# A hand-made instruction scheduler with the price of array shape changes by direction, traced durations, and a search over the finished order

## The chip, the cores and the metric

The kernel runs on one NeuronCore of a Trainium2 chip. Engines work side by side, each in the order of its own queue, and wait for each other by semaphores: TensorE (PE, matmuls; PEld is its weight load), VectorE (DVE), ScalarE (ACT), GpSimd (POOL) and SyncE (SP), which here issues nearly all DMA transfers. The metric is device time of one execution in microseconds (us), median of several runs.

## What is computed

A retention layer for 8 batches and 8 heads (sequence 576, head size 64) and, on its result, a two-layer network with a PReLU between.

```python
scores = scale * np.matmul(q, k.transpose(0, 1, 3, 2))
gamma = 1.0 - 2.0 ** (-5.0 - np.arange(H, dtype=np.float32))
Dmat = np.where(rel >= 0, gamma[:, None, None] ** rel[None, :, :], 0.0)
ret = scores * Dmat[None, :, :, :]
attn_out = np.matmul(ret, v)              # (8, 8, 576, 64)
x = attn_out.transpose(0, 2, 1, 3).reshape(4608, 512)
h = x @ w_in                              # (4608, 2048)
g = np.maximum(h, 0.0) + alpha * np.minimum(h, 0.0)
return g @ w_out                          # (4608, 512)
```

## The kernel before

**The work.** The attention is done in chunks of 64 positions. The first two batches go by `part_...` functions (all heads of a stretch at once), the other 24 pairs of batch and two heads by `joint` (L893): one joint computes scores and states of pair n (small matmuls of 64x64 at L913, L920, L923, one scheduler operation called "su") and the values of pair n-1 (128x64 matmuls at L861, two operations "v0" and "v1"). "su" fills the PSUM banks psa, the values fill psh. DVE masks the scores into the tile `at` (L941), ACT and DVE add up the states (`su`, L953 to L964), and SP's transfers copy qT into `at` and the states `su` into `vn`. Sixteen transfers belong to a joint, loads of the next pairs among them.

The network works on blocks of 256 tokens and slices of 256 hidden units. For 32 bits of precision each operand is split into three pieces (`h`, `l`, `d`; `split_g`, `split_roll`, `split_w`), and the products of pieces add up in PSUM. `unit_roll` (L1188) and `unit_two` (L1222) make the hidden units, in psh for one half of a slice and in psa for the other; `second` (L1340) multiplies by w_out into the banks pso; `evacuate` writes `o` (DVE L1358, L1363) and sends it out through SP. While weights are still on their way, the first eight cells use whole fp32 operands instead (`unit_plain` L1091, `second_plain` L1122); `convert` (L711) turns the 64-bit weights into fp32 on ACT, DVE and POOL. At about 440 us the attention is finished, and what follows are 128x512 matmuls alone.

**The order.** Nothing is issued as the functions are called. `do` records an `Op`: its engine, a cost in us that is written beside it, the operations that it depends on, the PSUM banks, whether it holds the port that DVE and POOL share (`lock`), its number of PE instructions (`size`), and a `kind` (for PE: "small" for 64-wide matmuls, "pieces" for the split 128x512 ones, "PE" for the rest). `dues` (L232) lays all operations out backwards from the end and so gives each a due time. `plan` (L266) goes forwards: for each engine it takes, among the ready operations that could start within a small slack of the earliest, the one with the least due time. A change of kind on PE costs a flat 0.1 us:

```python
SLACK, SWITCH = {"PE": 0.2}, {"PE": 0.1}
return t + SWITCH.get(op.eng, 0.0) * (kinds[op.eng] != op.kind)
```

A transfer is also held back by `plan` until its due time less 30 us, and until no more than 2 us of transfers are queued. Blocks of 256 PE instructions are modelled as fetched in 3.1 us (`CHUNK`, `FETCH`). Twelve rounds of `dues` and `plan` and then 243 random shifts of due times in stretches of 40 us keep the plan that ends first. Its order is issued on all engines; dependencies between holders of the port, and a limit on bytes in flight during the first 100 us, are added on the way. Costs and due times live only in this planning; the chip sees the order of each queue and the waits.

Of the kernel before, what the change touches and what calls it, by code (L numbers as in the profile page):

```python
# [1 line left out]

# [19 lines left out]
def kernel(  # L22
# [130 lines left out]
    ops, land = [], [LAND[0]]  # L153
# [48 lines left out]
        return op  # L202


    RATE, RATE_256, RATE_128 = 265e3, 205e3, 115e3

    def dma(to, fro, size, r, w, eng="SP", rate=RATE, hold=0.0):
        def f():
# [23 lines left out]
    def dues(after):  # L232
# [30 lines left out]
                    ready[d.eng].append(d)  # L263
        return due

    def plan(due):  # L266
        last = -min(due)
        left = [len(op.deps) for op in ops]
        ready = {e: [] for e in BEGIN}
        rest = [op.n for op in ops if op.eng == "PE"]  # L270
        end, begin, order = [0.0] * len(ops), [0.0] * len(ops), []
        free, held, port, wire, kinds = dict(BEGIN), {}, [0.0, ""], 0.0, {e: e for e in BEGIN}
        can = [0.0] * len(ops)

        at = [CHUNK - 190, 0.0]
        for op in ops:
            if not op.deps:
                ready[op.eng].append(op)

        def earliest(op):  # L280
            t = max(free[op.eng], can[op.n], op.hold)
            for b in op.banks:
                if b in held:
                    t = max(t, max([x + LAT.get(e, 0.1) for e, x in held[b].items()
                                    if e != op.eng] or [0.0]))
            if op.lock and port[1] != op.eng:
                t = max(t, port[0])
            if op.late:
                t = max(t, wire - BACKLOG, due[op.n] + last - HOLD)
            if op.size and at[0] + op.size > CHUNK:  # L290
                t = max(t, at[1] - op.cost * (CHUNK - at[0]) / op.size)
            return t + SWITCH.get(op.eng, 0.0) * (kinds[op.eng] != op.kind)

        while len(order) < len(ops):
            pick = None
            for e, queue in ready.items():
                if not queue:
                    continue
                c = [(earliest(op), op) for op in queue
                     if e != "PE" or op.n <= rest[0] + AHEAD_PE]  # L300
                if not c:
                    continue
                t0 = min(t for t, _ in c)
                t, op = min((x for x in c if x[0] <= t0 + SLACK.get(e, 0.05)),
                            key=lambda x: (due[x[1].n], x[1].n))
                if pick is None or t < pick[0]:
                    pick = t, op
            t, op = pick
            ready[op.eng].remove(op)
            if op.eng == "PE":  # L310
                rest.remove(op.n)
            begin[op.n] = t
            kinds[op.eng] = op.kind
            free[op.eng] = end[op.n] = t + op.cost
            if op.size:
                at[0] += op.size
                if at[0] >= CHUNK:
                    at[0] -= CHUNK
                    over = end[op.n] - op.cost * at[0] / op.size
                    at[1] = over + FETCH + min(max(wire - over, 0.0), 0.8)  # L320
            if op.late:
                wire = max(wire, t + op.cost) + op.late
# [12 lines left out]
        total = max(end)  # L335
        return total, order, begin, end

    AHEAD_PE = 150
    WINDOWS, STRETCH, TRIES, ROUNDS = 27, 20.0, 9, 9
    CHUNK, FETCH = 256, 3.1  # L340
    BACKLOG, HOLD = 2.0, 30.0
    LAG, HOLD_X = 2, 100.0
    X_TWO, QUICK, NQUICK, WDVE = 12, 13, 2, 16
# [1 line left out]
    EARLY, JOINTS = 1, {(s, i): 1 for s in range(14) for i in range(2) if (s, i) not in ((0, 0), (8, 1), (10, 1), (13, 0), (13, 1))}  # L345
    PUMP0, PUMP = ((1, 2), (0, 1), (0, 1), (0, 1)), ((1, 2), (1, 2), (0, 1), (0, 1))
    GROUPS = (("v0",), ("v1",), ("x", "su"))
    SLACK, SWITCH = {"PE": 0.2}, {"PE": 0.1}
    BEGIN = {"PE": 1.9, "ACT": 0.5, "DVE": 5.5, "POOL": 5.4, "SP": 0.5}


# [137 lines left out]
    def part_scores(x, bank):  # L489
# [7 lines left out]
        for m in range(2):  # L497
            def f(m=m):
                for c in range(NPAIR):
                    for p2 in range(2):  # L500
                        for h2 in range(2):
                            j = chunk(2 * m + p2)
                            nc.tensor.matmul(
                                ps[h2].get()[half(p2), (2 * c + m) * C:(2 * c + m + 1) * C],
                                kT()[half(h2), c, j], qT()[half(h2), c, j], start=True, stop=True)
            do("PE", 0.58, f, [(kt, "t", m), (qt, "t", m)], [(ps[0], m), (ps[1], m)], kind="small",
               size=64)
        for h2 in range(2):
            def g(h2=h2):
# [6 lines left out]
    def part_states(x, bank):  # L516
# [4 lines left out]
        for m in range(2):  # L521
            def f(m=m):
                for c in range(NPAIR):
                    for p2 in range(2):
                        for h2 in range(2):
# [3 lines left out]
                                             start=(m == 0 and c == 0),  # L529
                                             stop=(m == 1 and c == NPAIR - 1),  # L530
                                             skip_group_check=True)
            do("PE", 0.58, f, [key_p(x, 0, m), key_p(x, 2, m)], [(pu[0], 0), (pu[1], 0)], kind="small",
               size=64)
        for j in range(4):
            was = sums_key(x, j - 1) if j else carry_key(x) if x % 3 else None
# [24 lines left out]
    def part_values(x, bank):  # L560
# [7 lines left out]
        for m in range(2):  # L568
            def f(m=m):
                for c in range(NPAIR):  # L570
                    for p2 in range(2):
                        for h2 in range(2):
# [6 lines left out]
            do("PE", 0.58, f, [key_p(x, 2, m), (a, "m", 0), (a, "m", 1)], [(pv[0], 0), (pv[1], 0)],  # L579
               kind="small", size=64)  # L580


# [55 lines left out]
    def last_part(x):  # L638
# [28 lines left out]
        do("PE", 0.6, f, [(t, "t")], [(ps[0], 0), (ps[1], 0)], kind="small", size=32)  # L667
# [6 lines left out]
        def f():  # L674
# [6 lines left out]
            for c in range(NPAIR):  # L681
                for h2 in range(2):
                    for e in range(0, D, 32):
# [4 lines left out]
        do("PE", 1.25, f, [key_p(x, 2, 0), (t, "m", 0), (t, "m", 1), (t, "t"), carry_key(x)], [(pv, 0)],  # L688
           kind="small", size=96)
        gx, o = chunk_home(x, NJ - 1)  # L690
        do("ACT", 0.37, lambda: nc.scalar.copy(
# [158 lines left out]
    def values(n, pv):  # L850
# [6 lines left out]
        for i, js in enumerate((range(0, j1), range(j1, NJ))):  # L857
            def f(i=i, js=js):
                for j in js:
                    for h2 in range(2):  # L860
                        nc.tensor.matmul(pv[i].get()[half(h2), (j - js[0]) * C:(j - js[0] + 1) * C],  # L861
                                         vns[n % 2][:, h2, j], mt.get()[:, h2, j], start=True,
                                         stop=True)
            parts.append((0.133 * len(js), f, [(vn, x, h2) for x in "vs" for h2 in range(2)] +
                          [(mt, x, h2) for h2 in range(2) for x in ("q", "s", "x")],
                          [(pv[i], 0)]))
        return parts, lambda: keep_x(n, pv, j1)
# [18 lines left out]
    def on_pe(parts, groups):  # L886
        for some in groups:
            do("PE", sum(parts[x][0] for x in some), lambda some=some: [parts[x][1]() for x in some],
               [key for x in some for key in parts[x][2]],
               [key for x in some for key in parts[x][3]], kind="small",  # L890
               size=sum(136 if x == "su" else 72 if x[0] == "v" else 0 for x in some))

    def joint(n):  # L893
# [23 lines left out]
        def f():  # L917
            for j in range(NJ - 1):
                for h2 in range(2):
# [3 lines left out]
                    nc.tensor.matmul(chunks(uu)[half(h2), j], kn.get()[half(1 - h2), j],  # L923
                                     vns[n % 2][half(1 - h2), h2, j], start=True, stop=True,
                                     skip_group_check=True)
        parts["su"] = (1.09, f, [(kT, 0), (qT, 0), (kn, 0), (kn, 1), (vn, "v", 0), (vn, "v", 1)],
                       [(ss, 0), (uu, 0), (uu, 1)])
        on_pe(parts, [some for some in ([x for x in group if x in parts] for group in GROUPS)
                      if some])
# [90 lines left out]
    def split_x(vis, rooms=None, side=0):  # L1020
# [23 lines left out]
        late = vis["n"] >= LATE_X and rooms is None  # L1044
        for n in range(2):
            for c in parts(n, (0,)):
                do("ACT", 0.64 if len(c) > 1 else 0.38,
                   lambda c=c, to=view(0, c): nc.scalar.mul(piece(to()), raw(c), BELOW * 2.0 ** -12),
                   keys, key(0, c))
            for c in parts(n, (0, 1, 2)):  # L1050
# [8 lines left out]
                        out=piece(l()), in0=raw(c), in1=ht(), op=ALU.subtract),  # L1059
                        keys + [(h, 0)], key(1, c))  # L1060
                else:
                    do("ACT", 0.64 if wide else 0.38,
                       lambda c=c, d=d: nc.scalar.mul(piece(d()), raw(c), BELOW), keys, key(2, c))
# [5 lines left out]
                do("POOL", 1.29 if wide else 0.7,  # L1069
                   lambda l=l, d=d, h=view(0, c): nc.gpsimd.tensor_tensor(  # L1070
                       out=piece(d()), in0=h(), in1=l(), op=ALU.subtract),
                   key(0, c) + key(1, c), key(2, c), lock=True)
# [139 lines left out]
    def unit_two(va, vb, u, outs, f):  # L1212
# [3 lines left out]
        def mm():  # L1216
            for p, l in ((p0, 0), (p1, 2), (p0, 1)):
                for cc in range(NCC):
# [5 lines left out]
        do("PE", 2.73, mm, x_keys(va, 0) + x_keys(vb, 1) +  # L1224
           [w_at[u, i][l] for i in range(2) for l in range(3)], [(p0, 0), (p1, 0)], size=24, kind="pieces")
        fc = 2 * u + f
        for cols, gens, g in outs:
# [97 lines left out]
    def second(cell):  # L1325
# [7 lines left out]
        for m in range(2):  # L1333

            terms = ((0, 0), (0, 1)), ((1, 2),)
            for some in reversed(terms) if cell["last"] else (sum(terms, ()),):
                def mm(m=m, a=list(acc), some=some):
                    for f in range(2):
                        for b, l in some:
# [2 lines left out]
                                             w_piece(u, 2 + f, l),  # L1342
                                             start=(cell["first"] and f == 0 and l != 1),
                                             stop=(cell["last"] and f == 1 and l > 0))
                do("PE", 0.459 * len(some), mm, [(g, l) for _, l in some] +
                   [w_at[u, i][l] for i in (2, 3) for _, l in some],
                   [(acc[2 * m + b], 0) for b in sorted({b for b, _ in some})], size=4 * len(some), kind="pieces")
            if cell["last"]:
# [349 lines left out]
    for n in range(ROUNDS * WINDOWS):  # L1698
# [6 lines left out]
        if made[0] <= best[0]:  # L1705
            best, due = made, other

    port = None
    for op in best[1]:
        now[0] = best[2][op.n]  # L1710
        ins = op.fn()
        if op.lock:
            if port and port[0] != op.eng:
# [34 lines left out]
```

## Time and profile before

| | us |
|---|---|
| median of 3 runs | 918.88 (918.88 to 920.27) |
| profiled execution | 919.19 |
| its span | 917.4 |
| PE busy | 906.9 |
| PE weight loads (PEld) busy | 737.8 |
| DVE / ACT / POOL busy | 548.0 / 503.9 / 520.2 |
| data moved by DMA | 121.32 MB |

The span is the time from the first to the last instruction of the profiled execution. A line of the order of time gives start, duration, engine, source line, operation, output tile and input tiles, shapes and a count; in square brackets stands how long the engine was idle before it and what ended that. Rows are merged where the same instruction repeats, so their durations overlap: the time between two starts is the time that PE took. A row of stretches gives the stretch, its length, and for PE, PEld, DVE, ACT and POOL the busy time and (x) the number of instructions, then the clock granted to PE as a share of full speed, the busy share of the DMA engines and GB/s.

These groups take most of PE's time:

```profile
L1340 PE MATMUL pso<-w,g 128*128 128x512 f32 x1392 | 338.8, 391 | 0.0
L1188 PE MATMUL psh<-lx_x,w 128*128 128x512 f32 (+1 forms) x360 | 86.6, 379 | 0.0
L1188 PE MATMUL psa<-lx_x,w 128*128 128x512 f32 (+1 forms) x360 | 85.4, 376 | 0.0
```

### The profile page before, as it was taken

To read this page: it belongs to the slowest core of one execution; us is meant where nothing else is said; L and a number is where in the kernel's file an instruction comes from. 1 tells how busy PE (TensorE), PEld (TensorE's weight loads), DVE (VectorE), ACT (ScalarE), POOL (GpSimd) and SP (SyncE) were. 2 spreads that over 40 slices of the span, in tenths; PEclk is the share of its full clock that TensorE was granted. 3 is DMA by queue.
4 is the path that set the end of the run, shared out by engine and by line. 5 is a ranking of instruction groups with operands and counts; after the bars stand their busy time and mean duration, and the time that the engine had idled before them with its cause. 6 is when DMAs were issued, how large, how long until landed. Compare 5 with 4: busy or idle time off the path is not lost. (4 is left out here: it accounts for less than half of the span.)

```text
span 917.4 us, 19097 instructions
## 1 busy us (share of the span) xinstructions
PE 906.9 (99%) x7289; PEld 737.8 (80%) x7289; DVE 548.0 (60%) x1003; ACT 503.9 (55%) x1010; POOL 520.2 (57%) x461
## 2 busy tenths in 40 slices
PE   7999999999999999999999999999999999999998
PEld 6767688887888888888888888888888888888886
DVE  5786766667677667676757776344444534344343
ACT  4575455646565656565746555537463636364441
POOL 4776746456466665674542244665656656574624
PEclk9999999999999999999999999999999999999999
DMA  9995688977988879895243332212121322211112
GB/s 216 251 235 86 164 189 186 198 178 155 221 192 194 209 166 201 193 189 181 93 138 130 102 125 65 86 57 81 58 89 56 99 73 86 74 64 47 47 46 69
DMA packets 235947, 121.32 MB, mean 132 GB/s; under 512 B 203456, under 2 KB 203728, under 8 KB 235856
## 3 DMA queue, kind: packets, MB, share of 16 engines
q1 hardware_dynamic: 235712, 119.98, 52.1%
q8 instruction: 57, 0.93, 0.4%
q14 instruction: 34, 0.28, 0.1%
q10 hardware_dynamic: 144, 0.13, 0.0%
HBM read 74.19 MB, written 32.51 MB: 116 GB/s over the span
## 5 line engine op out<-in xcount | busy, mean ns | idle before, releaser
L1340 PE MATMUL pso<-w,g 128*128 128x512 f32 x1392 | 338.8, 391 | 0.0
L1340 PEld LDWEIGHTS pso<-w,g 128*128 128x128 f32 x1392 | 258.9, 188 | 55.2 <-POOL g L1267 1.2
L1264 POOL TENSOR_TENSOR g<-ga_all,g 128x512 fp32r<-128x512 f32 x76 | 97.9, 1291 | 130.4 <-ACT g L1260 105.0
L1267 POOL TENSOR_TENSOR g<-g 128x512 fp32r<-128x512 f32 x114 | 147.4, 1294 | 23.7 <-DVE su L1066 5.7
L1188 PE MATMUL psh<-lx_x,w 128*128 128x512 f32 (+1 forms) x360 | 86.6, 379 | 0.0
L1188 PE MATMUL psa<-lx_x,w 128*128 128x512 f32 (+1 forms) x360 | 85.4, 376 | 0.0
L1188 PEld LDWEIGHTS psa<-lx_x,w 128*128 128x128 f32 x360 | 65.1, 188 | 13.1 <-issue 0.4
L1188 PEld LDWEIGHTS psh<-lx_x,w 128*128 128x128 f32 x360 | 64.2, 188 | 12.9
L1260 ACT ACTIVATE g<-ga_all 128x512 fp32r<-128x512 f32 x76 | 47.6, 631 | 43.0 <-PE pso L1340 21.0
L1256 POOL TENSOR_TENSOR g<-g 128x512 fp32r<-128x512 f32 x22 | 28.5, 1296 | 64.0 <-DVE g L1253 38.3
L1264 POOL TENSOR_TENSOR g<-vn,g 128x512 fp32r<-128x512 f32 x25 | 32.4, 1297 | 37.5 <-ACT g L1260 34.9
L1340 PE MATMUL pso<-lx_x,g 128*128 128x512 f32 x216 | 53.5, 390 | 0.1
L1163 POOL TENSOR_TENSOR lx_x<-lx_x 128x512 fp32r<-128x512 f32 x28 | 35.9, 1294 | 26.0 <-DVE lx_x L1160 26.0
L941 DVE SCALAR_TENSOR_TENSOR at<-psa,pf,mask 64x512 f32<-64x512 f32 x48 | 36.0, 749 | 21.1 <-PE psh L861 10.2
L1340 PEld LDWEIGHTS pso<-lx_x,g 128*128 128x128 f32 x216 | 40.4, 188 | 9.0 <-DVE o L1363 0.7
L1262 ACT ACTIVATE g<-ga_all 128x512 fp32r<-128x512 f32 x76 | 47.2, 621 | 0.0
L1358 DVE TENSOR_TENSOR op<-pso,op 128x512 f32<-128x512 f32 x35 | 24.0, 686 | 31.3 <-PE pso L1340 31.2
L1202 ACT COPY ga_all<-psh 128x512 f32<-128x512 f32 (+1 forms) x30 | 16.7, 558 | 39.1 <-PE psh L1188 37.4
L861 PEld LDWEIGHTS psh<-at,vn 128*64 128x64 f32 x864 | 27.9, 137 | 8.7 <-issue 3.6
L1222 PE MATMUL psh<-w,w 128*128 128x512 f32 x144 | 34.6, 389 | 0.0
L1222 PE MATMUL psa<-w,w 128*128 128x512 f32 x144 | 34.6, 389 | 0.0
L754 POOL TENSOR_TENSOR wa<-wa,op 128x512 int32<-128x512 int32 x16 | 21.0, 1311 | 23.1 <-DVE wa L751 19.1
(329 smaller groups left out, 1883.3 us busy)
## 6 DMA issues: line engine op xcount, KB each, us to landing
xk<-x SPq DMA_DIRECT2D x18, 512.0 KB, 3.7
ok<-o SPq DMA_DIRECT2D x36, 256.0 KB, 2.9
op<-ok SPq DMA_DIRECT2D x18, 512.0 KB, 3.9
out_dram<-o SPq DMA_DIRECT2D x35, 256.0 KB, 2.3
x<-xk SPq DMA_DIRECT2D x16, 512.0 KB, 5.6
qx<-in_q_dram SPq DMA_DIRECT2D x96, 72.0 KB, 3.4
kx<-in_k_dram SPq DMA_DIRECT2D x96, 72.0 KB, 3.3
kn<-in_k_dram SPq DMA_DIRECT2D x48, 144.0 KB, 3.4
```

Of the source, the lines that this page charges most:

```text
L861: nc.tensor.matmul(pv[i].get()[half(h2), (j - js[0]) * C:(j - js[0] + 1) * C], vns[n % 2][:, h2, j], mt.get()[:, h2, j], start=True, stop= ...
L941: nc.vector.scalar_tensor_tensor(out=mt.get()[half(1 - h2), h2, j], in0=fro[x], scalar=pf[x, 1, h:h + 1], in1=mask[x, None, :].to_broadcas ...
L1163: do("POOL", 1.29, lambda h=h, l=l, d=d: nc.gpsimd.tensor_tensor(out=piece(d()), in0=h(), in1=l(), op=ALU.subtract), [(g, 0, n), (g, 1, n) ...
L1188: nc.tensor.matmul(out_of(p), w[:, c0:c0 + P], xp(l, cc), start=(l != 1 and cc == 0), stop=(l > 0 and cc == NCC - 1))
L1222: nc.tensor.matmul(p.get(), w[:, c0:c0 + P], piece(words_of(g)[:, o:o + DM]), start=(l != 1 and cc == 0), stop=(l > 0 and cc == NCC - 1))
L1256: do("POOL", 1.29, lambda: nc.gpsimd.tensor_tensor(out=piece(to.get()[:, 2]), in0=to.get()[:, 0], in1=to.get()[:, 1], op=ALU.subtract), [( ...
L1260: do("ACT", 0.64, lambda: nc.scalar.mul(piece(to.get()[:, 2]), whole(), BELOW), both, [(to, 2)])
L1262: do("ACT", 0.64, lambda: nc.scalar.mul(piece(to.get()[:, 0]), whole(), BELOW * 2.0 ** -12), both, [(to, 0)])
L1264: do("POOL", 1.29, lambda: nc.gpsimd.tensor_tensor(out=piece(to.get()[:, 1]), in0=whole(), in1=to.get()[:, 2], op=ALU.subtract), both + [( ...
L1267: do("POOL", 1.29, lambda: nc.gpsimd.tensor_tensor(out=piece(to.get()[:, 2]), in0=to.get()[:, 0], in1=to.get()[:, 1], op=ALU.subtract), [( ...
L1340: nc.tensor.matmul(a[2 * m + b].get(), piece(g.get()[:, l, f, m * P:(m + 1) * P]), w_piece(u, 2 + f, l), start=(cell["first"] and f == 0 a ...
L1358: do("DVE", 0.69, lambda: nc.vector.tensor_tensor(out=t(), in0=p1.get(), in1=t(), op=ALU.subtract), [(p1, 0)], [tk])
```

## The change

Three things. First, a change of kind on PE has a price by direction: from a large kind ("PE", "pieces") to a small one 0.09, from a small one to a large one 0.24, among small ones 0.1, between the two large kinds nothing. The values become a kind of their own ("values"). Second, costs are set to other figures: small matmuls, values, the split products, some narrow ACT and POOL operations, the rates of transfers. Third, `mend` takes the order that `plan` found. It replays a whole order of all engines with fixed positions, and tries 30000 moves of one operation to an earlier or later place. In 15% of them it puts a small PE operation next to another small one; in the others it picks a gap on PE, walks back along what caused it, and pulls an operation forward or pushes the one ahead of it back. A move stays if the measure, the end plus 0.3 times the mean start of PE's operations, is no worse. The replay has the fetch of instruction blocks, the banks, the port and the transfers' wire; it does not hold transfers back as `plan` does, and neither does the issue. `now`, which decides what the limit on bytes in flight is applied to, comes from the replay's start times. The arithmetic is untouched.

```diff
-    RATE, RATE_256, RATE_128 = 265e3, 205e3, 115e3
+    RATE, RATE_256, RATE_128 = 272e3, 211e3, 119e3
...
+    def switch(a, b):
+        if a == b or a in BIG and b in BIG:
+            return 0.0
+        return OUT if b in BIG else INTO if a in BIG else AMONG
...
-            return t + SWITCH.get(op.eng, 0.0) * (kinds[op.eng] != op.kind)
+            return t + switch(kinds[op.eng], op.kind)
...
+    def mend(order):
...
+        def earlier(x, p):
+            p = max([p] + [pos[d] + 1 for d, _ in needs[x]])
+            return p < pos[x] and (order[:p] + [x] + order[p:pos[x]] + order[pos[x] + 1:], p, pos[x])
+
+        def later(x, p):
+            p, q = min([p, num - 1] + [pos[u] - 1 for u in uses[x]]), pos[x]
+            return p > q and (order[:q] + order[q + 1:p + 1] + [x] + order[p + 1:], q, p)
+
+        def proposal():
+            if rnd.random() < 0.15:
+                x = rnd.choice(some)
+                by, p, seen = rnd.choice((1, -1)), pos[x], 0
+                while seen < 14:
+                    p += by
+                    if not 0 <= p < num:
+                        return None
+                    if eng[order[p]] == pe:
+                        if small[order[p]]:
+                            return seen and (later(x, p - 1) if by > 0 else earlier(x, p + 1))
+                        seen += 1
+                return None
+            if not idle or rnd.random() < 0.02:
+                idle[:] = gaps()
+            x = rnd.choices(idle, [min(g, 1.0) for g, _ in idle])[0][1]
+            for _ in range(rnd.randrange(25)):
+                w = why[x] if why[x] >= 0 else before[x] if why[x] == -1 else (
+                    locked[x] if why[x] == -3 else -1)
+                if w < 0:
+                    break
+                x = w
+            y = before[x] if rnd.random() < 0.7 or not ops[x].lock else locked[x]
+            for _ in range(rnd.choice((0, 0, 0, 1, 1, 2, 3, 4))):
+                y = before[y] if y >= 0 and before[y] >= 0 else y
+            if y < 0:
+                return None
+            if rnd.random() < 0.5:
+                return earlier(x, pos[y])
+            return later(y, pos[x] + rnd.choice((0, 0, 0, 5, 10, 20, 40)))
...
+        def worth(total, begin):
+            return total + 0.3 * sum(begin[n] for n in on_pe) / len(on_pe)
+        value = worth(total, begin)
+        for _ in range(MOVES):
+            change = proposal()
+            if not change:
+                continue
+            other, first, last = change
+            k = first // MARK
+            b, e, w, m = begin[:], end[:], why[:], dict(marks)
+            t = replay(other, k * MARK, marks[k], b, e, w, m, (marks, end), last + 1)
+            if t is None:
+                continue
+            v = worth(t or total, b)
+            if v <= value:
+                order, begin, end, why, marks = other, b, e, w, m
+                total, value = t or total, v
+                index()
+        return order, begin, total
...
+    MARK, FAR, WORSE, MOVES = 64, 192, 0.3, 30000
...
-    SLACK, SWITCH = {"PE": 0.2}, {"PE": 0.1}
+    SLACK, BIG, INTO, OUT, AMONG = {"PE": 0.2}, ("PE", "pieces"), 0.09, 0.24, 0.1
...
-            do("PE", 0.58, f, [(kt, "t", m), (qt, "t", m)], [(ps[0], m), (ps[1], m)], kind="small",
+            do("PE", 0.49, f, [(kt, "t", m), (qt, "t", m)], [(ps[0], m), (ps[1], m)], kind="small",
...
-            parts.append((0.133 * len(js), f, [(vn, x, h2) for x in "vs" for h2 in range(2)] +
+            parts.append((0.117 * len(js), f, [(vn, x, h2) for x in "vs" for h2 in range(2)] +
...
-               [key for x in some for key in parts[x][3]], kind="small",
+               [key for x in some for key in parts[x][3]], kind="values" if some[0][0] == "v" else "small",
...
-        parts["su"] = (1.09, f, [(kT, 0), (qT, 0), (kn, 0), (kn, 1), (vn, "v", 0), (vn, "v", 1)],
+        parts["su"] = (1.07, f, [(kT, 0), (qT, 0), (kn, 0), (kn, 1), (vn, "v", 0), (vn, "v", 1)],
...
-                do("PE", 0.459 * len(some), mm, [(g, l) for _, l in some] +
+                do("PE", 0.4545 * len(some), mm, [(g, l) for _, l in some] +
...
+    mended = mend([op.n for op in best[1]])
     port = None
-    for op in best[1]:
-        now[0] = best[2][op.n]
+    for n in mended[0]:
+        op = ops[n]
+        now[0] = mended[1][n]
         ins = op.fn()
```

More of the change, by code (lines that the diff above doesn't have):

```diff
@@ L1 @@
+import random
 from contextlib import ExitStack
@@ L336, in plan, with replay, index, gaps @@
         return total, order, begin, end
+    def mend(order):
+        num, rnd = len(ops), random.Random(1)
+        engs = list(BEGIN)
+        pe = engs.index("PE")
+        eng = [engs.index(op.eng) for op in ops]
+        kind = [op.kind for op in ops]
+        small = [op.eng == "PE" and op.kind not in BIG for op in ops]
+        kinds = {k for e, k in zip(eng, kind) if e == pe} | {"PE"}
+        turn = {(a, b): switch(a, b) for a in kinds for b in kinds}
+        lat = [LAT.get(e, 0.1) for e in engs]
+        needs = [[(d.n, wait(d, op)) for d in op.deps] for op in ops]
+        uses = [[u.n for u in users[op.n]] for op in ops]
+        on_pe = [n for n in range(num) if eng[n] == pe]
+        some = [n for n in on_pe if small[n]]
+        def replay(order, at, state, begin, end, why, marks, was=None, same=0):
+            free, port, side, wire, a0, a1, kd, held = state
+            free, held = list(free), {b: dict(v) for b, v in held.items()}
+            for p in range(at, num):
+                if p % MARK == 0:
+                    st = list(free), port, side, wire, a0, a1, kd, {b: dict(v) for b, v in held.items()}
+                    if was and p >= same:
+                        if st == was[0][p // MARK] and all(
+                                end[m] == was[1][m] or all(pos[u] < p for u in uses[m])
+                                for m in order[at:p]):
+                            return 0.0
+                        if p >= same + FAR and free[pe] > was[0][p // MARK][0][pe] + WORSE:
+                            return None
+                    marks[p // MARK] = st
+                n = order[p]
+                op, e = ops[n], eng[n]
+                t, w = free[e], -1
+                if op.hold > t:
+                    t, w = op.hold, -2
+                for d, x in needs[n]:
+                    if end[d] + x > t:
+                        t, w = end[d] + x, d
+                for b in op.banks:
+                    for q, (x, m) in held.get(b, {}).items():
+                        if q != e and x + lat[q] > t:
+                            t, w = x + lat[q], m
+                if op.lock and side != e and port > t:
+                    t, w = port, -3
+                if e == pe:
+                    if op.size and a0 + op.size > CHUNK:
+                        t = max(t, a1 - op.cost * (CHUNK - a0) / op.size)
+                    t += turn[kd, kind[n]]
+                    kd = kind[n]
+                begin[n], why[n] = t, w
+                f = free[e] = end[n] = t + op.cost
+                if e == pe and op.size:
+                    a0 += op.size
+                    if a0 >= CHUNK:
+                        a0 -= CHUNK
+                        over = f - op.cost * a0 / op.size
+                        a1 = over + FETCH + min(max(wire - over, 0.0), 0.8)
+                if op.late:
+                    end[n] = wire = max(wire, f) + op.late
+                for b in op.banks:
+                    held.setdefault(b, {})[e] = f, n
+                if op.lock and (side == e or f > port):
+                    port, side = f, e
+            return max(end)
+        def index():
+            last, lock = [-1] * len(engs), -1
+            for i, n in enumerate(order):
+                pos[n], before[n], last[eng[n]] = i, last[eng[n]], n
+                if ops[n].lock:
+                    locked[n], lock = lock, n
+        def gaps():
+            f = 0.0
+            for n in order:
+                if eng[n] == pe:
+                    if begin[n] - f > 0.05:
+                        yield begin[n] - f, n
+                    f = begin[n] + ops[n].cost
+        def earlier(x, p):
[30 more added lines that the diff above has]
+            if y < 0:
+                return None
+            if rnd.random() < 0.5:
+                return earlier(x, pos[y])
+            return later(y, pos[x] + rnd.choice((0, 0, 0, 5, 10, 20, 40)))
+        pos, before, locked = [0] * num, [-1] * num, [-1] * num
+        begin, end, why, marks, idle = [0.0] * num, [0.0] * num, [-1] * num, {}, []
+        state = [BEGIN[e] for e in engs], 0.0, -1, 0.0, CHUNK - 190, 0.0, "PE", {}
+        index()
+        total = replay(order, 0, state, begin, end, why, marks)
+        def worth(total, begin):
[15 more added lines that the diff above has]
+                total, value = t or total, v
+                index()
+        return order, begin, total
@@ L531, in f @@
                                              skip_group_check=True)
-            do("PE", 0.58, f, [key_p(x, 0, m), key_p(x, 2, m)], [(pu[0], 0), (pu[1], 0)], kind="small",
+            do("PE", 0.49, f, [key_p(x, 0, m), key_p(x, 2, m)], [(pu[0], 0), (pu[1], 0)], kind="small",
                size=64)
@@ L578, in f @@
                                              skip_group_check=True)
-            do("PE", 0.58, f, [key_p(x, 2, m), (a, "m", 0), (a, "m", 1)], [(pv[0], 0), (pv[1], 0)],
+            do("PE", 0.49, f, [key_p(x, 2, m), (a, "m", 0), (a, "m", 1)], [(pv[0], 0), (pv[1], 0)],
                kind="small", size=64)
@@ L666, in f @@
                                      start=True, stop=True)
-        do("PE", 0.6, f, [(t, "t")], [(ps[0], 0), (ps[1], 0)], kind="small", size=32)
+        do("PE", 0.5, f, [(t, "t")], [(ps[0], 0), (ps[1], 0)], kind="small", size=32)
         for h2 in range(2):
@@ L687, in f @@
                                          skip_group_check=True)
-        do("PE", 1.25, f, [key_p(x, 2, 0), (t, "m", 0), (t, "m", 1), (t, "t"), carry_key(x)], [(pv, 0)],
+        do("PE", 1.1, f, [key_p(x, 2, 0), (t, "m", 0), (t, "m", 1), (t, "t"), carry_key(x)], [(pv, 0)],
            kind="small", size=96)
@@ L1046, in split_x @@
             for c in parts(n, (0,)):
-                do("ACT", 0.64 if len(c) > 1 else 0.38,
+                do("ACT", 0.62 if len(c) > 1 else 0.405,
                    lambda c=c, to=view(0, c): nc.scalar.mul(piece(to()), raw(c), BELOW * 2.0 ** -12),
@@ L1061, in split_x @@
                 else:
-                    do("ACT", 0.64 if wide else 0.38,
+                    do("ACT", 0.62 if wide else 0.405,
                        lambda c=c, d=d: nc.scalar.mul(piece(d()), raw(c), BELOW), keys, key(2, c))
@@ L1068, in split_x @@
                         keys + key(2, c), key(1, c), lock=True)
-                do("POOL", 1.29 if wide else 0.7,
+                do("POOL", 1.29 if wide else 0.745,
                    lambda l=l, d=d, h=view(0, c): nc.gpsimd.tensor_tensor(
@@ L1223, in mm @@
                                      start=(l != 1 and cc == 0), stop=(l > 0 and cc == NCC - 1))
[L1224 removed]
+        do("PE", 2.721, mm, x_keys(va, 0) + x_keys(vb, 1) +
            [w_at[u, i][l] for i in range(2) for l in range(3)], [(p0, 0), (p1, 0)], size=24, kind="pieces")
```

## The prediction

> **What bounds the kernel now.** I read the page first, then busy time by stretches, then the order of time on PE around small matmuls, then what waits on SP's queue.
>
> ```profile
> span 917.4 us, 19097 instructions
> PE 906.9 (99%) x7289; PEld 737.8 (80%) x7289; DVE 548.0 (60%) x1003; ACT 503.9 (55%) x1010; POOL 520.2 (57%) x461
> ```
>
> PE is busy for 99% and no other engine for more than 60%. Only what PE does or waits for can change the time. The stretches say where PE is not full (the first two figures are the length of the stretch and PE's busy time):
>
> ```profile
> 0.00:25.00 25.00, 20.06 (x429) 17.14 (x429) 15.26 (x58) 11.10 (x18) 13.21 (x26) 1.00 0.96 222
> 25.00:50.00 25.00, 23.69 (x395) 17.41 (x395) 18.65 (x32) 14.49 (x27) 16.39 (x16) 1.00 1.03 243
> 50.00:105.00 55.00, 54.88 (x820) 37.66 (x818) 45.27 (x86) 32.90 (x67) 40.54 (x36) 1.00 0.70 155
> 105.00:300.00 195.00, 194.85 (x2160) 159.20 (x2159) 133.95 (x256) 112.16 (x239) 109.01 (x88) 1.00 0.85 188
> 600.00:800.00 200.00, 200.00 (x884) 165.64 (x883) 89.45 (x146) 102.11 (x201) 120.10 (x111) 1.00 0.22 72
> ```
>
> PE stands idle for 4.94 us before 25, for 1.31 from 25 to 50, and hardly at all up to 900. The clock is 1.00 throughout. From 440 on there are only 128x512 matmuls, which start every 0.227 us (884 in 200 us); nothing that an order can do helps there. So the change can earn only in the first 50 us, in the changes between large and small matmuls up to 440, and in the last 18 us.
>
> What a change of shape costs is read from starts, because busy time hides it. First a joint whose small matmuls stand together, then one that is cut in two:
>
> ```profile
> 299.17 4.24 PE L1340 MATMUL pso<-w,g 128*128 128x512 f32 x18
> ...
> 304.54 1.27 PE L861 MATMUL psh<-at,vn 128*64 128x64 f32 x36
> 305.73 1.20 PE L1188 MATMUL psh<-lx_x,w 128*128 128x512 f32 x4
> 306.77 1.54 PE L1340 MATMUL pso<-w,g 128*128 128x512 f32 x6
> ```
>
> ```profile
> 337.67 2.43 PE L1340 MATMUL pso<-w,g 128*128 128x512 f32 x10
> 340.03 0.92 PE L861 MATMUL psh<-at,vn 128*64 128x64 f32 x24
> 340.88 1.66 PE L1340 MATMUL pso<-w,g 128*128 128x512 f32 x6
> ...
> 343.66 0.57 PE L861 MATMUL psh<-at,vn 128*64 128x64 f32 x12
> 344.16 2.11 PE L1188 MATMUL psh<-lx_x,w 128*128 128x512 f32 x8
> ```
>
> The 18 large ones should end at 299.17 + 18 x 0.2272 = 303.26; the first small one starts at 303.34 (0.08 late). After the run, 4 large ones take 1.04 and not 0.91 (0.13 late). The whole excursion costs 305.73 - 303.26 + 0.13 = 2.60. The cut one goes from 337.67 + 10 x 0.2272 = 339.94 to 344.16, and 0.13 more; less the 6 large ones in between (1.36) that is 2.99. One cut costs **0.39 us**. The joint at 235 is cut in three: by the same sum its pieces come to 3.20, 0.30 a cut.
>
> **The change part by part.** No instruction is added or removed: the 19097 stay, with the same tiles and the same 16 SP transfers per joint. Only the order on each queue moves, and with it the waits that follow from buffers, the port lock and the bytes in flight. The corrected durations cost nothing on the chip; they act through the order too, since the plan is made anew before the search starts.
>
> *1. Cut joints, 105 to 440.* Going through PE's order of time I count 31 runs of small matmuls from 102 on, seven of them second or third pieces of one joint (142, 211, 223, 237, 240, 342, 359). The old planner priced every change of kind at 0.1, so cutting was nearly free to it; the new price, 0.09 in and 0.24 out, is about what the rows show (0.08 + 0.13, and some 0.15 before the first large start). Both the greedy plan and the search, which picks small operations for 15% of its moves and puts them next to another run, now work against cuts. Lower bound: 0 (the pieces were apart because psh or psa was not free, and still are). Upper: 7 x 0.39 = 2.7. I take six cuts at 0.33 (between 0.30 and 0.39): **2.0**.
>
> *2. Runs before 102.* There are 21, of parts whose scores, states and values depend on each other through a mask on DVE. Perhaps five can join a neighbour, 5 x 0.33 = 1.7 at most. But two such blocks are 256 instructions (128 weight loads and 128 matmuls) in some 2.3 us, and PE's queue stalls in just such places:
>
> ```profile
> 15.86 0.34 PE L574 MATMUL pso<-g,w 64*64 64x64 f32 x7 [1.32 <-issue]
> ...
> 30.49 0.27 PE L599 MATMUL psa<-w,w 64*64 64x64 f32 x2 [1.03 <-ACT spy L588]
> 31.57 0.21 PE L599 MATMUL psh<-w,w 64*64 64x64 f32 x1 [0.28 <-issue]
> ```
>
> The two stalls by "issue" fall on PE's records 449 and 1217, which are 3 x 256 apart: a block of instructions comes late, I read. A joint of 208 instructions among large matmuls does not fill a block so fast, so part 1 is spared. A pair joined here saves 0.33 and may pay 0.28. Bounds -0.5 and 1.7; I take **0.3**, nearer to the row that stalls. [...]
>
> *3. Waits before 50 us.* Of the 6.25 us, 1.69 are the start. The named waits are 0.69 and 0.42 for POOL's scaling (w L455, itself waiting for loads), 0.32 for the DVE mask, 1.32 and 0.28 by issue, 0.43 for a weight conversion at 23.1, and 1.03 for ACT's spy copy, which runs at 30.29 behind a weight conversion (L732, from 29.75) and a plain unit's ACT step. That last wait is a matter of order on ACT, and large matmuls could also fill it; moving it earns 1.03 less at most one excursion (0.33), so 0.7. Of the other 3.46 I take 0.4, because the DMA engines are busy for 0.96 and 1.03 of these stretches and no order makes a load land sooner than its bytes allow. **1.1**; bounds 0 and 2.9.
>
> *4. The end.* PE waits before the last cell:
>
> ```profile
> 907.90 3.02 PE L1284 MATMUL pso<-w,g 128*128 128x512 f32 x12 [0.17 <-POOL g L1256]
> ```
>
> Its weight load stood 0.59. The chain of waits goes back through POOL (1.29), DVE and ACT to a g buffer that PE itself frees at 904.85; the order can help only by letting PE free it sooner. **0.2**; bounds 0 and 0.6.
>
> *5. New waits.* A search that moves single operations until a model just holds leaves no margin where the model is short. One joint has none already:
>
> ```profile
> 221.42 1.15 PE L861 MATMUL psh<-at,vn 128*64 128x64 f32 x30 [0.15 <-DMA vn<-su]
> ```
>
> Four more such waits would be 0.6. Bounds 0 (the search also pulls producers forward, since its measure counts the mean start of PE's work) and 6.0 (the second rival). I take **-0.6**.
>
> Sum: 2.0 + 0.3 + 1.1 + 0.2 - 0.6 = 3.0 us. The profiled execution took 919.19 (span 917.4 and 1.79 around it) and would take 916.2; the median of the runs, 918.88, lies 0.31 below it, so on that scale the forecast is **915.9**.
>
> **The rivals.** *More than that.* If all cuts go (2.7), the early pairs join without stalls (1.2), half of the early waits go (2.0) and the end gives 0.3 with 0.2 lost: 6.0 gained, **912.9**. For it: PE has nothing but order against it in the first 105 us, and 30000 moves are many. Against: the loads of the first 50 us.
>
> *Slower: values wait for transfers.* SP's queue runs in order, and today it stands behind output stores:
>
> ```profile
> SPq L209 <- DVE o L1363: 349.8, 48, 19.3
> ```
>
> That is 48 waits of 7.3 us in the mean. Behind such a store are the copies at<-qT and vn<-su, and for these the values of the next joint wait on PE; PE's own order is fixed, so all matmuls behind stand too. If the search puts a store, or a load that waits for a buffer, ahead of these copies with just the modelled margin, and they land 0.25 us late (the row at 221.42 shows 0.15) on each of 24 joints, 6.0 us go: 918.9 - 3.6 + 6.0 = **921.3**. It decides above 0.23 us a joint (3.6 + 1.84 over 24). Against it: in the trace only one of 24 joints waits at all, and the copies take 3.4 to 3.5 us from issue to landing where a joint comes every 13.5.
>
> *Nothing to speak of.* The cuts stay, because a whole joint needs both psh and both psa banks at once and the units' drains on ACT and DVE hold them, and the anew made plan gives back at the start what it gains: 0.7 us in all, **918.2**. For it: PE is full from 50 on, and 3.0 is a third of one per cent.
>
> **How the numbers follow.** A difference of 0.2% (1.84 us) is about what a measurement of this kernel can tell from none; faster begins at 917.04, slower above 920.72. Chances: the forecast 0.48 (its own range 914.3 to 917.3, a small part of it above 917.04), more 0.17, nothing 0.17, slower 0.18. Faster: 0.46 + 0.17 + 0.03 from the edge of "nothing" = 0.66; same 0.02 + 0.14 = 0.16; slower 0.18. The bounds of the terms reach from 911.0 (2.7 + 1.7 + 2.9 + 0.6) to 925.4 (6.0 + 0.5); the range is 912.4 to 919.8: some 5% left out below, some 15% above, where a part of the slower case lies.
>
> **What will show it.** Runs of small matmuls on PE: 24 or 25 from 102 on in place of 31 if part 1 is right; if 30 or more, it is wrong. Waits of over 0.1 us before L861 by DMA vn<-su or at<-qT: none to four if term 5 is right, over ten for the slower rival. Before 50, PE's busy time up by about a microsecond, and the spy wait of 1.03 shorter. "Issue" stalls among the early small blocks up by one or two if the block reading holds. From 440 to 900, no difference at all: the stretch 600 to 800 keeps its 884 matmuls. The forecast is wrong if PE shows new gaps after 105 us, or if the first 50 us lose more than 2 us.

## The result and the profile after

The changed kernel takes 922.42 us (median of 10 runs, 920.41 to 924.01) against 919.37 for the kernel before, run beside it (10 runs, 918.82 to 921.55). The ratio is **1.0028**, 95% interval 1.0017 to 1.0039: slower by 0.28%, where 0.32% faster was forecast. A ratio is taken over all runs and can differ a little from that of the two medians. The profiled execution took 922.73, its span grew from 917.4 to 921.0.

The page of the changed kernel (line numbers grow by 152 from before in the functions that matter here, by 1 ahead of the new code):

```profile
span 921.0 us, 19121 instructions
PE 907.1 (98%) x7289; PEld 737.2 (80%) x7289; DVE 550.0 (60%) x1003; ACT 502.7 (55%) x1010; POOL 519.4 (56%) x461
```

The five engines have the same numbers of instructions as before, and PE the same busy time within 0.2 us: what was added is waiting. (The prediction held the total at 19097; the 24 more are all waits for semaphores.) The stretches of the changed kernel say where (length of the stretch, PE's busy time, then the other engines):

```profile
0.00:25.00 25.00, 20.05 (x368) 17.35 (x369) 18.63 (x61) 11.55 (x19) 12.79 (x25) 1.00 0.97 242
25.00:50.00 25.00, 23.44 (x397) 16.82 (x395) 16.86 (x30) 13.04 (x24) 16.29 (x16) 1.00 0.99 227
50.00:105.00 55.00, 52.75 (x840) 35.97 (x838) 42.10 (x77) 32.27 (x63) 39.52 (x34) 1.00 0.72 152
105.00:300.00 195.00, 193.95 (x2195) 158.02 (x2185) 135.30 (x263) 111.71 (x240) 111.48 (x90) 1.00 0.86 190
```

PE is idle for 4.95, 1.56, 2.25 and 1.05 us, 9.81 in all; before it was 4.94, 1.31, 0.12 and 0.15, or 6.52. That is 3.3 of the span's 3.6 us, and two thirds of it fall between 50 and 105 us, where the kernel before had no gap to speak of. PE's waits in the changed kernel (total, times, longest) name them:

```profile
PE pso L726 <- issue: 1.5, 1, 1.5
PE pso L631 <- POOL w L607: 1.3, 1, 1.3
PE psa L1075 <- issue: 1.0, 1, 1.0
PE psh L1065 <- DVE at L1093: 1.0, 1, 1.0
PE psa L804 <- ACT x L783: 0.7, 1, 0.7
PE psa L631 <- ACT x L843: 0.6, 1, 0.6
PE psa L655 <- ACT op L637: 0.5, 1, 0.5
PE psa L631 <- ACT w L637: 0.4, 1, 0.4
PE psa L751 <- ACT spy L740: 0.2, 1, 0.2
```

The first two have counterparts before (1.3, and 1.1 in two). The spy wait is 0.2 in place of 1.0. Six of 0.4 us or more are new: four for ACT that sum to 2.2 and one of 1.0 for a DVE mask, all ahead of 106 us, and 1.0 by issue at 158.9. How one of them comes about, in ACT's and then PE's order of time:

```profile
50.32 0.67 ACT L882 ACTIVATE w<-w 128x512 f32<-128x512 f32 x1 [1.76 <-DMA w<-in_moe_w_out_dram]
50.89 0.57 ACT L637 COPY op<-psa 128x512 f32<-128x512 f32 x1
```

```profile
52.00 0.27 PE L655 MATMUL psa<-op,w 64*64 64x64 f32 x1 [0.52 <-ACT op L637]
```

ACT's queue stands for 1.76 us at the first step of a weight conversion whose load has not landed. Behind it, in order, stand the two copies of transposes that PE's next scores need. The wait of 0.6 (at 46.5 us) has the same cause: ACT stood 3.95 us for a weight load ahead of that copy. The one of 0.4 (at 70.0) stands behind a conversion step that had its load, and the one of 0.7 (at 38.9) behind a copy that had itself waited for PE. The mask stood behind a DVE operation that waited 0.77 us for POOL.

### The profile page after: what moved, and what is told of

It reads as the page before. It is cut to its first block, busy times and chain, and to the rows that moved or that the text cites. A ratio compares the mean times of both kernels' runs of the same rounds, so it can differ in the third digit from the quotient of the medians.

```text
span 921.0 us, 19121 instructions
## 1 busy us (share of the span) xinstructions
PE 907.1 (98%) x7289; PEld 737.2 (80%) x7289; DVE 550.0 (60%) x1003; ACT 502.7 (55%) x1010; POOL 519.4 (56%) x461
## 4 chain that ended last, share of the span: by engine, by line
PE 89%; POOL 3%; DMA 2%; DVE 2%; issue 2%; SPq 1%; ACT 0%; POOLq 0%; DVEq 0%; ACTq 0%
PE pso L1492 39%; PE psh L1374 12%; PE psa L1374 12%; PE psh L1340 9%; PE psa L1340 8%; PE psh L1013 3%; PE psa L1075 2%; POOL w L937 2%; PE pso L1274 1%; DVE w L939 1%; DMA w<-in_moe_w_out_dram 1%; PE psa L1072 1%; PE psh L1243 1%; DMA w<-in_moe_w_in_dram 1%; PE psh L1065 1%
```

## The experiments

The kernel before was run again beside each group of kernels, and its median lay between 918.87 and 919.59; so the ratio is what is compared. For most of them the order of the kernel before was written out as a list of 3802 operation numbers, `FIRST_ORDER`, and handed to the changed code in place of the new plan's order; the rounds of planning are then left out.

**Is it the plan or the search?** Two theories stood against each other: S, that the loss comes with the plan, which is made anew from the new prices and durations before the search starts; M, that it comes with the search, which uses up slack.

`no_search`:

```diff
-    MARK, FAR, WORSE, MOVES = 64, 192, 0.3, 30000
+    MARK, FAR, WORSE, MOVES = 64, 192, 0.3, 0
```

> The changed kernel with 0 moves in place of 30000: new prices and durations, the order as the plan made it. Theory S (the loss comes with the new plan, whose first 110 us are worse than the old plan's; the search repairs a part of it): slower than the changed kernel or like it, 922 to 926. Theory M (the loss comes with the search, which uses up slack that the model does not know it needs): near the kernel before, 918 to 920.5.

Measured 924.12, ratio 1.0045 (1.0032 to 1.0058). Without the search the changed kernel looks slower still, though the two intervals overlap a little. Its trace, of one of its faster executions (921.37), has waits of the same sort, on ACT's weight conversions and on loads, but of the six named above only the 0.7 is among them:

```profile
PE pso L1274 <- ACT w L882: 1.4, 1, 1.4
PE pso L631 <- DMA w<-in_k_dram: 1.1, 1, 1.1
PE psa L804 <- ACT x L783: 0.7, 1, 0.7
PE psa L631 <- DMA w<-in_k_dram: 0.5, 1, 0.5
```

`old_order_replayed` and `search_old`, with 0 and with 30000 moves:

```diff
-    mended = mend([op.n for op in best[1]])
+    mended = mend(FIRST_ORDER)
```

> The order of the kernel before, written into the changed code, with 0 moves. A control: both theories expect the time of the kernel before, 918.5 to 920.5. If it is over 921, the way of issuing (which transfers the limit on bytes in flight is put on) is the cause and not the order.

Measured 918.95, ratio 0.9992 (0.9983 to 1.0001). The way of issuing plays no part that can be told here; the order makes the time. Its profile is a second one of the old order, and it shows what differs between executions of one order:

```profile
PE pso L825 <- issue: 1.9, 1, 1.9
PE psa L850 <- ACT spy L839: 0.2, 1, 0.2
```

The spy wait is 0.2 here and was 1.0 before, with no operation moved. PE is idle for 5.92 us up to 25 and for 0.33 from there to 50: other places, but the same sum of 6.25.

> The same 30000 moves, but from the order of the kernel before. S: faster than before, by about what the switches are worth (2 us) and perhaps a microsecond of early waits: 915.5 to 918. M: slower than before, 921 to 924, with new waits on ACT, DVE and transfers.

Measured 917.45, ratio **0.9981** (0.9963 to 1.0000). The same search from the old order gains 0.19%, about what it gains from the new plan (1.0028 against 1.0045). M expected a loss in this run, so M falls. The stretches of `search_old`:

```profile
0.00:25.00 25.00, 21.27 (x493) 18.26 (x493) 16.95 (x59) 10.51 (x17) 13.49 (x26) 1.00 1.06 236
25.00:50.00 25.00, 24.47 (x401) 17.77 (x397) 19.51 (x34) 16.28 (x29) 17.67 (x16) 1.00 1.03 249
50.00:105.00 55.00, 54.60 (x766) 37.50 (x762) 45.39 (x85) 32.17 (x65) 39.96 (x35) 1.00 0.69 147
```

Idle: 3.73, 0.53 and 0.40. Of new waits its list has one, 0.3 for `su`:

```profile
PE pso L825 <- issue: 1.1, 1, 1.1
PE pso L730 <- POOL w L706: 0.8, 2, 0.5
PE psa L1439 <- DVE su L1215: 0.3, 1, 0.3
PE psa L850 <- ACT spy L839: 0.2, 1, 0.2
```

`search_old_late`, the search shut out of the first 106 us:

```diff
             other, first, last = change
+            if first < 501:
+                continue
```

> As the last, but only moves behind the 501st operation of the order (after about 106 us) are allowed, so that the first part is the old one word for word. S: 916 to 918, the switches alone. M: 920 to 922 if the slack is used up there too; no more than 919.5 if it is used up only where transfers are dense, before 106 us.

Measured 918.12, ratio 0.9993 (0.9977 to 1.0009): no difference that can be told. The point estimate lies 0.1% above `search_old`, so the search may earn more in the first 106 us than behind them, but the intervals overlap, and the granted clock differs too: it was 0.998 or less in ten of these twelve executions and in two of `search_old`'s twelve. In the executions at 0.999 or 1.000 the means are 916.97 (two) and 917.25 (ten).

**Which part of the order?** Two hybrids, each a valid order: one kernel's first operations, and the rest in the other's order, without moves. In words the edit is this; in the kernels the list that is handed in is again called `FIRST_ORDER`:

```diff
-    mended = mend([op.n for op in best[1]])
+    mended = mend(OLD_FIRST_501 + REST_AS_CHANGED)    # the other: NEW_FIRST_478 + REST_AS_BEFORE
```

> The first 501 operations (some 106 us) in the order of the kernel before, all others in the order of the changed kernel, 0 moves. If the loss sits in the first 106 us (theory S): 916.5 to 919, at least 3 us faster than the changed kernel. If the changed rest has its share by the instruction stall at 157 us that its trace shows: 918.5 to 920.

Measured 920.43, ratio 1.0020 (1.0006 to 1.0034).

> The mirror image: the changed kernel's first 478 operations, then the old order. S: 920.5 to 924, as slow as the changed kernel or slower by the 1.9 us of switches that the old rest has. If it is under 920 the loss sits after 106 us.

Measured 920.05, ratio 1.0010 (1.0000 to 1.0021). So S in its strict form, all of the loss before 106 us, was wrong: I expected the first hybrid at 919 or under. Each half seems to carry a part, though the second interval reaches 1.0000. In the first hybrid's profile PE is idle for 0.54 us from 105 to 300, where the replay of the old order has none, and 0.44 of that is the changed kernel's stall by issue, now at 157.8. The larger gaps are at its start:

```profile
PE pso L825 <- issue: 2.5, 1, 2.5
PE psh L1656 <- POOL ident masks.py:199: 1.7, 1, 1.7
PE pso L730 <- POOL w L706: 1.4, 2, 0.9
PE psa L1174 <- issue: 0.4, 1, 0.4
```

```profile
0.00:25.00 25.00, 18.86 (x421) 16.45 (x421) 13.83 (x54) 10.07 (x17) 11.18 (x24) 0.93 1.01 222
```

The order there is the old one, whose own profile has 1.3 at this place and whose replay (`old_order_replayed`) has 1.9. The granted clock is 0.93 in this stretch, 1.00 in the profile before. It differs between the kernels compared, too: the first hybrid had 0.998 or less in ten of twelve executions, the second in one of twelve, the kernel before in 19 of 29. At like clock the halves change places. At 0.999 or 1.000 the second hybrid takes 920.28 in the mean (11 executions) against 918.83 before (10), 1.5 us more. At 0.997 and 0.998 the first takes 920.44 (7) against 919.32 (17), 1.1 us more. So the new start costs at least as much as the new rest, and part of the first hybrid's 0.2% goes with the clock; the samples are small.

**Why is the new plan worse?** Theory C: the old figures are a picked point of a rough landscape, and any other figures, better founded or not, give an ordinary plan. Theory F: the new figures mislead. Two kernels move one figure of the kernel before a little; both are without the search.

```diff
-    SLACK, SWITCH = {"PE": 0.2}, {"PE": 0.1}
+    SLACK, SWITCH = {"PE": 0.2}, {"PE": 0.09}
```

> The kernel before with one figure of its planner moved by a tenth: a change of kind costs 0.09 in place of 0.1; no search over the finished order. Theory C (the old figures are a picked point of a rough landscape, and any other figures, better founded ones too, give an ordinary plan): slower than before by 2 to 6 us, 921 to 925. Theory F (the new figures themselves mislead the plan): within 1 us of the kernel before, 918 to 920.

Measured **926.24**, ratio 1.0075 (1.0062 to 1.0088). A hundredth of a microsecond in one price of the planner costs some 7 us. The waits of this kernel:

```profile
PE psa L574 <- DVE w L541: 1.8, 1, 1.8
PE psh L1405 <- POOL ident masks.py:199: 1.7, 1, 1.7
PE psa L479 <- DMA w<-in_k_dram: 1.3, 1, 1.3
PE psh L861 <- DVE ga_all L1203: 0.7, 1, 0.7
```

Again waits for loads and for the engines that prepare operands, at other places than in the changed kernel.

```diff
-    RATE, RATE_256, RATE_128 = 265e3, 205e3, 115e3
+    RATE, RATE_256, RATE_128 = 268e3, 207e3, 116.5e3
```

> The kernel before with its three transfer rates raised by about one per cent (268, 207 and 116.5 in place of 265, 205 and 115), which is half of what the change does to them; nothing else. Theory C (any other figures give an ordinary plan): 921 to 927. Theory F (the size of the new figures matters): 918 to 920.

Measured 921.26, ratio 1.0021 (1.0011 to 1.0032). `old_seed2` has `RandomState(2)` for `RandomState(1)` in the kernel before:

> The kernel before with another seed for the random shifts of due times in its planning, all figures as they were. If it is the figures that make the old plan good (theory C with the figures as what was picked): 918 to 920, like the kernel before. If the seed was what was picked: 921 to 926.

Measured 920.31, ratio 1.0015 (1.0001 to 1.0029): a little slower, at the edge of what can be told, and between the two ranges expected. The seed alone lost 0.15%, two small moves of the figures 0.21% and 0.75%, and the change, which moves some twenty figures at once, 0.45% (`no_search`). The first two cannot be told apart, so the old plan is a good point of figures and seed together; with one other seed, which of them counts for more stays open. Both theories agree that the new plan is worse; that a hundredth and one per cent do harm of the same size as well founded corrections speaks for C.

**Is there a figure still wrong?** The whole fp32 products stand at 1.86 us in the planner, where their starts in the traces give 8 x 0.216 and 4 x 0.429, or 1.73 and 1.72. So the replay should have PE later than it is before 106 us; no profile shows the replay's times.

```diff
-            do("PE", 1.86, mm, keys + [plain[4 * u + cc]], [(ph, 0)], size=16)
+            do("PE", 1.73, mm, keys + [plain[4 * u + cc]], [(ph, 0)], size=16)
...
-            do("PE", 1.86, mm, [(ga, 0), (ga, 1), plain[4 * u + 2], plain[4 * u + 3]],
+            do("PE", 1.73, mm, [(ga, 0), (ga, 1), plain[4 * u + 2], plain[4 * u + 3]],
```

> The changed kernel with one more duration corrected: the whole fp32 products of the first 106 us (unit_plain, second_plain) cost 1.73 in place of 1.86; the traces show 8 x 0.216 and 4 x 0.429 us. Theory D (the changed kernel's new waits before 106 us come from PE being faster than its model there, so that producers on ACT and DVE are ordered for a later PE): 915 to 919, and fewer PE waits for ACT between 38 and 106 us. Theory C: another ordinary draw, 919 to 924.

Measured 919.62, ratio 1.0006 (0.9997 to 1.0016): better than the changed kernel, outside theory D's range, inside theory C's. PE's longest wait is now another:

```profile
PE psa L726 <- DVE w L693: 2.1, 1, 2.1
PE pso L631 <- POOL w L607: 1.3, 2, 0.8
PE psa L804 <- ACT x L783: 0.6, 1, 0.6
```

The same correction where no plan is made anew, in the replay of `search_old`:

> search_old with the whole fp32 products at 1.73 in place of 1.86, in the replay alone (the order that it starts from is the old one). Theory D (producers before 106 us are ordered for a PE that is later than the real one): 915 to 917, faster than search_old's 917.45. If the correction is worth nothing on the chip: 917 to 918.

917.23, ratio 0.9978 (0.9969 to 0.9986).

> The same with another seed of the search. It shows how far two searches from one order lie apart: within 1 us of the last if the search's gain is robust, further if each is a draw of its own.

917.73, ratio 0.9990 (0.9981 to 0.9999). Around `search_old`'s 0.9981: the correction is worth nothing that can be told from the draw of the search, and D is not shown.

**Do the prices by direction help the search?** From the old order, with a flat price in the replay, and each with a second seed:

```diff
-    SLACK, BIG, INTO, OUT, AMONG = {"PE": 0.2}, ("PE", "pieces"), 0.09, 0.24, 0.1
+    SLACK, BIG, INTO, OUT, AMONG = {"PE": 0.2}, ("PE", "pieces"), 0.1, 0.1, 0.1
```

> search_old with the flat 0.1 for each change between small and large matmuls in the replay, so that the search does not know the direction's prices. If its gain comes from these prices: 918 to 919.5. If it comes from moving operations out of waits: 916.5 to 918, with fewer joints made whole.

Measured **915.40**, ratio 0.9971 (0.9954 to 0.9989), the best of all. Its stretches:

```profile
0.00:25.00 25.00, 21.03 (x461) 17.86 (x461) 16.59 (x58) 10.84 (x18) 12.84 (x26) 1.00 1.04 230
25.00:50.00 25.00, 24.55 (x408) 17.92 (x412) 19.51 (x34) 15.90 (x28) 17.83 (x18) 1.00 1.05 250
50.00:105.00 55.00, 55.00 (x801) 38.10 (x791) 45.08 (x85) 32.52 (x67) 39.13 (x34) 1.00 0.72 150
```

Idle for 3.97, 0.45 and 0.00: the first 50 us give 1.8 of the 4.0 us by which its span (913.4) is shorter than the one before. It has 27 runs of small matmuls from 102 us on, `search_old` 28, the kernel before 31; at 0.33 to 0.39 the four fewer would be another 1.3 to 1.6 us (an estimate). The price by direction is not needed to take cuts away: here a flat one and the moves that put small matmuls together were enough.

> search_old_flat with another seed of the search. If the flat price really lets the search do better: 915 to 916.5, at least 1 us faster than search_old_seed2. If search_old_flat was a lucky draw: 917 to 918.5.

916.85, ratio 0.9976 (0.9962 to 0.9990).

> search_old with that other seed and the prices by direction. 917 to 918 if the first draw (917.45) was typical; 915 to 916.5 if draws scatter more than prices do.

917.73, ratio 0.9977 (0.9966 to 0.9988). So flat 0.9971 and 0.9976, by direction 0.9981 and 0.9977: the kind of price cannot be told from the draw.

> Both: the flat price and 1.73 for the whole fp32 products, in the replay, from the old order. If both gains are real and separate: 914.5 to 915.5. If each is mostly draw: 915.5 to 918.

918.38, ratio 0.9982 (0.9964 to 1.0000). Nothing adds up: gains of single draws are not separate gains. All seven searches from the old order over its whole length came out under the kernel before, by 0.10% to 0.29%; two of their intervals reach 1.0000.

## Why the prediction was wrong

**The step that failed** is the sentence ahead of the terms: "The corrected durations cost nothing on the chip; they act through the order too, since the plan is made anew before the search starts." I named the new plan and then gave it no term, and took each term from the old order as if the search started there. `no_search` measures what was left out: +0.45%, 4.1 us of 918.87 (by the medians 5.25). Against this the search brings 0.17% (1.0045 to 1.0028) here and 0.19% from the old order, or 1.6 to 1.7 us, about half of the 3.0 that my terms gave.

*Cut joints (2.0).* Wrong here. I asked for 24 or 25 runs from 102 us on and called 30 a failure; the changed kernel has 30. The new price in the plan alone takes none away, `no_search` has 31. From the old order the search left 28, so three or four cuts of seven go, about 1.1 us at 0.33.

*Runs before 102 (0.3).* 17 in place of 21, so four excursions, 1.3 us, were saved at once by the plan itself (`no_search` has 17 too). From the old order the search joins none: `search_old` and `search_old_flat` keep 21. No second early stall by issue came of it. But I said that a joint is spared, and the changed kernel stands for 1.0 us inside one.

*Waits before 50 us (1.1).* The spy wait went from 1.0 to 0.2, but `old_order_replayed` has 0.2 with the old order as well. So that fall is no proof of the argument, and the 0.7 that I took for it had been read from a wait that differs between executions. The stretch as a whole lost 0.26 us of busy time here (idle 6.25 to 6.51), with less work done in it. From the old order it gained 1.99 (6.25 to 4.26), more than I took.

*The end (0.2).* PE's gap before the last cell went from 0.55 us to 0.48, start to start, where 0.227 is usual: 0.07 won.

*New waits (-0.6).* The mis-sized term. The six named above make 4.2 us (2.2 + 1.0 + 1.0), not one of them for the copies vn<-su or at<-qT. Waits of this sort come with the new plan: before 105 us PE is idle for 8.7 us in the profile of `no_search`, for 8.8 in that of the changed kernel and for 6.4 in that of the kernel before. The search put other waits in their place and did not clear them. From the old order, where the search has the same freedom, there is 0.3 of that sort. So the search's hunger for slack, which I gave as the reason, does not explain the loss by itself.

Two signs came out as the prediction set them: the stretch 600 to 800 keeps its 884 matmuls, and a new gap after 105 us (1.05 at 158.9) marks the forecast as wrong.

The slower rival came out on the right side and by the wrong mechanism: in-order queues do hold up what PE needs, but they are those of ACT (0.5 and 0.6 us behind weight loads, two of the four waits) and DVE (1.0), and no value matmul waits for SP's copies. That 922.4 lies near its 921.3 is luck. The rival called "nothing to speak of" had the true cause in half a sentence, that the plan made anew gives back what the search gains, without a price.

## What to carry to other kernels

When an edit changes figures that a planner with ties and thresholds works from, the whole order is drawn anew; price that draw on its own, by moving one figure by a per cent and running the result, before any term of the intended gain. Here four such draws without a search came out 0.15 to 0.75% slower than the plan in hand, and the intended gain was 0.3%. Refine the best order in hand, not a new one: seven searches from the old order made the kernel 0.1 to 0.3% faster.

## What the runs showed that was not expected

In 17 of the 18 traces PE stalls by issue, for 0.2 to 2.5 us, at its record 449 (weight loads, matmuls and semaphore instructions of PE's queue counted from 0), in whatever operation that is. All 30 stalls by issue over 0.1 us sit at 449 plus a multiple of 256; the changed kernel's later one is at record 4545, which is 449 + 16 x 256. This is its line:

```profile
158.88 0.27 PE L1075 MATMUL psa<-vn,kn 64*64 64x64 f32 x1 [1.05 <-issue]
```

Its length is not set by the order: with the same first 501 operations it was 1.3, 1.9, 1.9 and 2.5 us in four profiles (before, `old_order_replayed`, `search_old_late`, `old_start_new_rest`). That a block of instructions comes late at these places is my reading of their distance, 256 records or a multiple of it. In the first 25 us the DMA engines are 0.96 to 1.06 busy; that the block waits behind loads there is my reading too. Neither was tested.

A lower clock goes with the three longer stalls. In these three profiles the granted clock is 0.93 in the first 25 us, and at the end of the stall or within a microsecond of it a stretch of some 3.4 us has a clock of 0.50 to 0.51; before, with 1.3, it has none. `old_seed2` and `old_price_009` show the same after gaps of 1.9 and 1.8 us at about 30 us (0.93 from 25 to 50 us in the second); `plain_173` does not after one of 2.1 us (1.00). What decides between them is open.
